# A quarter of each diagonal score block mirrored, mirrored tiles stored in twos, the stacked operand copied by GpSimd, and one router product two steps later

## Chip, cores and metric

The kernel runs on one core of a Trainium2 chip. The metric is the device time of one execution in microseconds (us), as the median of several runs.

## What is computed

The input is 8 batches of 1856 rows. An attention without softmax comes first, a mixture of 16 experts after it:

```python
scores = scale * np.matmul(z, z.transpose(0, 2, 1))     # z: 8 x 1856 x 64, scale = 1/1856
attn = np.maximum(scores, 0.0) ** 2
x = (u * np.matmul(attn, v)).reshape(14848, 256)
# router: best of 4 groups, then best of 4 experts in it, weight = both softmax values
# every row goes to its one expert e:
out[row] = weight * (np.maximum(x[row] @ w1[e], 0.0) @ w2[e])    # w1: 256 x 1024, w2: 1024 x 256
```

The matrix of scores is symmetric in each batch.

## The kernel before

**Tiles.** In each batch the 1856 queries are cut into four chunks, c = 0 to 3 (in batches 1 to 7: 512, 512, 512 and 320 wide), and the keys into 15 blocks of 128, k = 0 to 14 (the last has 64 new ones). One *step* is one key block of one chunk, so a batch has 60 steps. All fp32 values are split into a high and a low fp32r part, and each product is made of these parts.

**One step.** `scores(s)` makes the scores of a block: two matmuls (L365, L366) into one of three PSUM banks; ScalarE applies Relu (L369, tile `r`) and Square (L376); VectorE makes the high part `ah` (L377) and the low part `al` (L380). In steps that `ACT_TWICE` names, ScalarE squares twice and so makes `ah` as well (L373, L374), and VectorE's L377 falls away. `attn_v(s)` then has six matmuls (L402, L403, L405, two halves of the output's columns) that add `ah` and `al` times v to the output banks. `scores` runs six steps ahead of `attn_v` (`LEAD`). `zm` is the chunk's query operand: the high part of z in partitions 0 to 63, the low part in 64 to 127. It is put together in step 5 of the chunk before (L257) by two DMAs of the Sync queue, and has two buffers.

**Mirrored blocks.** In batches 1 to 7 a block below the diagonal is not computed. When a block above the diagonal is done, `put_mirror` (L302) transposes it in 32x32 tiles on VectorE (L305, tile `mt`) and the Sync queue stores it in DRAM (`sym`, L313). Seven steps before the mirrored block's turn, `load_mirror` (L315) loads four key blocks with four DMAs into an `at` tile (L321); ScalarE makes `ah` from it (L354) and VectorE `al` (L355). The order of the key blocks in a chunk stands in the table `KORD`. The diagonal blocks, key blocks 4c to 4c+3 of chunks 0 to 2, are computed whole.

**Buffers.** `r`, `ah`, `al`, `mt` and the parts of z share one ring `q` of 31 tiles of 2 KB per partition.

**Router.** At a chunk's end the product with u gives `xT`; `logits` (L472) makes the router's product on TensorE in PSUM tag `m`, which has one bank, `logits_out` (L480) empties it one step later, and `LG` (L492) says how many steps after the chunk's end this happens: 9 for the third chunk, which is step 8 of the fourth. The routing itself (`route`) is many small VectorE operations, a small product in the same bank `m` (L600), and scatters of rows into `bucket` by GpSimd's indirect DMAs (L637).

**Order.** From step 15 to step 464 TensorE, VectorE and ScalarE run their instructions in the order in which the program records them. The order of the Sync and GpSimd queues is set by a scheduler. Each engine works its queue in order. After step 479 come the 16 experts (`phase1`, `phase2_t`, L860), which the change doesn't touch.

Of the kernel before, what the change touches and what calls it, by code (L numbers as in the profile page):

```python
# [29 lines left out]
def tile_glu_attn_moe(  # L30
# [311 lines left out]
    def scores(s):  # L342
# [3 lines left out]
        for far in (ATL, 12):  # L346
            lb, lc, li = steps[min(s + far, NS - 1)]
            lk = key(lb, lc, li)
            if lk % KT == 0 and mirrored(lb, lc, lk) and ((lc, lk) == (3, 8) and lb < B - 1) == (far != ATL):
                load_mirror(lb, lk // KT, KB[lc])  # L350
        if mirrored(b, c, k):
            at = ats[(b, k // KT, KB[c])][:, k % KT]
            ah, al = new_z(f"ah_{s}")[:, 0:w], new_z(f"al_{s}")[:, 0:w]
            nc.scalar.copy(out=ah.rearrange("p (g x) -> p g x", x=32), in_=at)  # L354
            nc.vector.tensor_sub(  # L355
                out=al.rearrange("p (g x) -> p g x", x=32), in0=at, in1=f32(ah).rearrange("p (g x) -> p g x", x=32)
            )
# [891 lines left out]
```

## Time and profile before

| | |
|---|---|
| median of 3 runs | 1449.96 us (1449.88 to 1450.25) |
| the profiled execution's own time | 1449.4 us |
| its span, first to last instruction | 1447.6 us |
| mean granted TensorE clock | 0.998 of full speed |
| TensorE (PE) busy | 1436.9 us, 99% |
| VectorE (DVE) busy | 1137.4 us, 79% |
| ScalarE (ACT) busy | 926.1 us, 64% |
| GpSimd (POOL) busy | 284.3 us, 20% |
| DMA queue of Sync: share of the 16 DMA engines | 62.1% |

Busy time of TensorE counts pipelined matmuls, which overlap: one matmul's listed duration is longer than the distance from its start to the next one's. The attention takes the first 765 us or so, the experts the rest; shares over the whole span mix the two.

### The profile page before, as it was taken

To read this page: it belongs to the slowest core of one execution; us is meant where nothing else is said; L and a number is where in the kernel's file an instruction comes from. 1 tells how busy PE (TensorE), PEld (TensorE's weight loads), DVE (VectorE), ACT (ScalarE), POOL (GpSimd) and SP (SyncE) were. 2 spreads that over 40 slices of the span, in tenths; PEclk is the share of its full clock that TensorE was granted. 3 is DMA by queue.
4 is the path that set the end of the run, shared out by engine and by line. 5 is a ranking of instruction groups with operands and counts; after the bars stand their busy time and mean duration, and the time that the engine had idled before them with its cause. 6 is when DMAs were issued, how large, how long until landed. Compare 5 with 4: busy or idle time off the path is not lost.

```text
span 1447.6 us, 22265 instructions
## 1 busy us (share of the span) xinstructions
PE 1436.9 (99%) x7113; PEld 1240.4 (86%) x7113; DVE 1137.4 (79%) x2339; ACT 926.1 (64%) x1613; POOL 284.3 (20%) x351
## 2 busy tenths in 40 slices
PE   9999999999999999999999999999999999999997
PEld 7898888888888888888788999888888888999986
DVE  7889999999998998989988576776566666666663
ACT  8887887787878878778675354444445444444442
POOL 0002112220222203221114222111211221122122
PEclk9999999999999999999999999999999999999999
DMA  9997969979799797996975473554533545555421
GB/s 320 328 242 214 239 184 256 233 211 233 174 263 222 210 235 174 264 230 165 236 181 148 94 193 74 126 139 123 144 96 90 142 126 132 134 129 134 132 60 44
DMA packets 397656, 255.98 MB, mean 177 GB/s; under 512 B 241775, under 2 KB 352883, under 8 KB 397536
## 3 DMA queue, kind: packets, MB, share of 16 engines
q1 hardware_dynamic: 385712, 223.50, 62.1%
q0 software_dynamic: 11744, 30.90, 7.2%
q8 instruction: 56, 0.92, 0.3%
q14 instruction: 64, 0.52, 0.1%
q10 hardware_dynamic: 80, 0.13, 0.0%
HBM read 108.29 MB, written 89.21 MB: 136 GB/s over the span
## 4 chain that ended last, share of the span: by engine, by line
PE 99%; DVE 0%; ACT 0%; issue 0%; POOL 0%; POOLq 0%
PE yT L860 23%; PE o L402 14%; PE o L403 14%; PE o L405 13%; PE ph L787 8%; PE ph L786 8%; PE ph L788 8%; PE sc L365 5%; PE sc L366 5%; PE pl L478 1%; PE pl L477 1%; PE py L817 0%; PE warm_ps L913 0%; PE py L820 0%; PE pk L600 0%
## 5 line engine op out<-in xcount | busy, mean ns | idle before, releaser
L402 PE MATMUL o<-ah,vl 128*128 128x512 f32 (+2 forms) x960 | 354.4, 370 | 0.6 <-DVE ah L377 0.4
L403 PE MATMUL o<-ah,vh 128*128 128x512 f32 (+2 forms) x960 | 354.2, 369 | 0.0
L405 PE MATMUL o<-al,vh 128*128 128x512 f32 (+2 forms) x896 | 329.0, 369 | 0.0
L797 DVE SCALAR_TENSOR_TENSOR hl<-ph,hh 128x512 fp32r<-128x512 f32 (+12 forms) x288 | 173.8, 609 | 145.4 <-ACT hh L791 144.4
L860 PE MATMUL yT<-hh,w_e 128*128 128x512 f32 (+12 forms) x1120 | 269.3, 360 | 0.0
L791 ACT ACTIVATE hh<-ph 128x512 fp32r<-128x512 f32 (+12 forms) x288 | 153.5, 536 | 147.8 <-PE ph L788 144.9
L369 ACT ACTIVATE r<-sc 128x512 f32<-128x512 f32 (+2 forms) x312 | 178.6, 572 | 83.4 <-PE sc L366 80.4
L885 POOL DMA_INDIRECT out_dram<-y,meta x126 | 125.4, 995 | 496.4 <-DVE y L883 468.8
L860 PEld LDWEIGHTS yT<-hh,w_e 128*128 128x128 f32 x1120 | 200.1, 188 | 25.1
L637 POOL DMA_INDIRECT bucket<-rows,di x121 | 135.9, 1123 | 375.4 <-issue 217.3
L787 PE MATMUL ph<-xh_m,w1h_e 128*128 128x512 f32 (+12 forms) x576 | 207.3, 360 | 0.0
L402 PEld LDWEIGHTS o<-ah,vl 128*128 128x128 f32 x960 | 180.2, 188 | 30.6 <-DVE ah L377 0.8
L786 PE MATMUL ph<-xh_m,w1l_e 128*128 128x512 f32 (+12 forms) x576 | 206.4, 360 | 0.0
L403 PEld LDWEIGHTS o<-ah,vh 128*128 128x128 f32 x960 | 180.2, 188 | 29.0
L788 PE MATMUL ph<-xl_m,w1h_e 128*128 128x512 f32 (+12 forms) x576 | 202.8, 360 | 0.0
L380 DVE TENSOR_TENSOR al<-r,ah 128x512 fp32r<-128x512 f32 (+2 forms) x280 | 187.9, 671 | 17.3 <-PE sc L366 0.5
L405 PEld LDWEIGHTS o<-al,vh 128*128 128x128 f32 x896 | 167.9, 188 | 26.6 <-DVE al L380 0.7
L376 ACT ACTIVATE r<-r 128x512 f32<-128x512 f32 (+2 forms) x284 | 173.9, 612 | 9.0
L860 PE MATMUL yT<-hl,w_e 128*128 128x512 f32 (+12 forms) x560 | 159.1, 359 | 0.0
L863 ACT COPY yp<-yT 128x1024 uint16<-128x1024 uint16 (+2 forms) x70 | 59.3, 847 | 143.6 <-PE yT L860 104.9
L377 DVE CAST ah<-r 128x512 fp32r<-128x512 f32 (+2 forms) x284 | 117.8, 415 | 20.4 <-ACT r L376 14.6
L365 PE MATMUL sc<-zm,z2h 128*128 128x512 f32 (+2 forms) x312 | 120.1, 385 | 0.0
(164 smaller groups left out, 1964.3 us busy)
## 6 DMA issues: line engine op xcount, KB each, us to landing
raw_e<-in_w_dram SPq DMA_DIRECT2D x64, 512.0 KB, 6.4
sym<-mt SPq DMA_DIRECT2D x126, 256.0 KB, 4.2
at<-sym SPq DMA_DIRECT2D x84, 256.0 KB, 5.2
bucket<-padrow SPq DMA_DIRECT2D x32, 660.0 KB, 10.0
at<-sym SPq DMA_DIRECT2D x84, 160.0 KB, 5.9
vr<-in_v_dram SPq DMA_DIRECT2D x23, 512.0 KB, 5.3
ut<-in_uT_dram SPq DMA_DIRECT2D x23, 512.0 KB, 5.1
zr<-in_zT_dram SPq DMA_DIRECT2D x23, 256.0 KB, 8.6
```

What stands on the lines that cost most here:

```text
L365: held(nc.tensor.matmul(ps[:, 0:w], z2h[:, ks], zm, start=True, stop=False))
L369: held(nc.scalar.activation(out=a, in_=ps[:, 0:w], func=AF.Relu, scale=1.0 / S))
L376: held(nc.scalar.activation(out=a, in_=a, func=AF.Square))
L380: held(nc.vector.tensor_sub(out=al, in0=a, in1=f32(ah)))
L402: held(nc.tensor.matmul(o, vl[:, dsl], ah, start=(i == 0), stop=False))
L403: held(nc.tensor.matmul(o, vh[:, dsl], ah, start=False, stop=end and al is None))
L405: held(nc.tensor.matmul(o, vh[:, dsl], al, start=False, stop=end))
L786: nc.tensor.matmul(o, wt["l"][d][:, fs], xh[:, d, 0:W], start=(d == 0), stop=False)
L787: nc.tensor.matmul(o, wt["h"][d][:, fs], xh[:, d, 0:W], start=False, stop=False)
L788: nc.tensor.matmul(o, wt["h"][d][:, fs], xl[:, d, 0:W], start=False, stop=(d == ND - 1))
L797: nc.vector.scalar_tensor_tensor(out=dst, in0=o[:, c0:c1], scalar=0.0, in1=f32(hh[:, c0:c1]), op0=ALU.max, op1=ALU.subtract)
L860: nc.tensor.matmul(o, wt["2"][f // 2][:, w0:w0 + P], hs[f][q // 2][:, 0:n], start=((f, q) == (0, 0)), stop=((f, q) == (NF - 1, 2)))
```

## The change

Five things change together. The tables `KORD` and `ACT_TWICE` are new too; `ACT_TWICE` is now looked up by key block k, not by place in the chunk.

1. **Diagonal blocks.** In chunks 0 to 2 of batches 1 to 7, the third and fourth diagonal key blocks (k mod 4 = 2, 3) are computed for queries 256 to 511 of the chunk alone (`cut`, `w0`). Their first 256 columns are the mirror of what the first two diagonal blocks hold in columns 256 to 511. `put_diag` transposes that part (128x256) into a half of a `q` tile `dt`, and one DMA stores two of them (`dg`); `load_diag` loads them back, three steps ahead (`DGL`), with four DMAs into a tile `dl`. ScalarE and VectorE make `ah` and `al` from it in two more operations of 256 columns.
2. **Stores in twos.** Mirrored blocks with k below 12 are transposed into `st` tiles of 4 KB per partition, two blocks to a tile, and two such tiles exist (`NST`). One DMA of 512 KB stores both. Loads come in runs of 1 KB, not 512 bytes. Blocks 12 to 14 stay as they were.
3. **Ring.** The ring `q` has 27 tiles in place of 31.
4. **zm.** From chunk (1, 1) on, two GpSimd copies of 64 partitions put `zm` together, in place of two DMAs.
5. **Router.** `LG` of the third chunk is 11, not 9.

```diff
-    ACT_TWICE = ((4, 8, 12), (6, 10), (), ())
+    NST = 2
+    NQT = 27
+    ACT_TWICE = ((1, 6, 8, 9, 11), (5, 9, 12), (), ())
+    HALF = 256
+    DGL = 3
...
-                nc.sync.dma_start(f32(zm[0:DQ, dst]), f32(z2h[0:DQ, src]))
-                nc.sync.dma_start(f32(zm[DQ:P, dst]), f32(z2l[DQ:P, src]))
+                nc.gpsimd.tensor_copy(out=zm[0:DQ, dst], in_=f32(z2h[0:DQ, src]))
+                nc.gpsimd.tensor_copy(out=zm[DQ:P, dst], in_=f32(z2l[DQ:P, src]))
...
+    def put_duo(b, c, k, a):
+        cc, kk = k // KT, k % KT
+        pair = (b, KB[c], cc)
+        if (pair, kk % 2) not in duos:
+            duos[pair, kk % 2] = sb("st", [P, 1024], F32, NST, f"st_{b}_{c}_{k}").rearrange(
+                "p (j h t x) -> p h t j x", h=2, t=KT, x=32)
...
+        nc.vector.transpose(out=st[:, kk // 2], in_=a.rearrange("p (t j x) -> p t j x", t=KT, x=32))
+        if half:
...
+            nc.sync.dma_start(sym[pair][r0:r0 + P, :].rearrange("p (j h t x) -> p j h t x", h=2, t=KT, x=32),
+                              st.rearrange("p h t j x -> p j h t x"))
...
+    def half_diag(b, c, k):
+        return MB[0] <= b < MB[1] and c < NQ - 1 and k // KT == c
+
+    def put_diag(b, c, k, a):
...
+        t2 = dgs[(b, c)][:, kk * HALF:(kk + 1) * HALF]
+        nc.vector.transpose(
+            out=t2.rearrange("p (j t x) -> p t j x", t=2, x=32),
+            in_=a[:, HALF:512].rearrange("p (t j x) -> p t j x", t=2, x=32),
+        )
+        if kk == 1:
...
+            nc.sync.dma_start(
+                dgd[(b, c)].rearrange("(k p) w -> p k w", p=P),
+                dgs.pop((b, c)).rearrange("p (k w) -> p k w", k=2),
+            )
+
+    def load_diag(b, c):
+        at = new_zraw(f"dl_{b}_{c}").rearrange("p (g x) -> p g x", x=64)
+        src = dgd.pop((b, c)).rearrange("(g r) (j x) -> j r g x", r=32, x=64)
+        for j in range(4):
+            nc.sync.dma_start(at[j * 32:(j + 1) * 32], src[j])
...
     KORD = (
-        (0, 4, 1, 5, 2, 6, 3, 7, 8, 12, 9, 13, 10, 11, 14),
-        (0, 8, 1, 9, 2, 10, 3, 11, 4, 12, 5, 13, 6, 14, 7),
-        (12, 0, 13, 1, 14, 2, 8, 3, 9, 4, 10, 5, 11, 6, 7),
+        (0, 4, 1, 6, 5, 7, 8, 12, 10, 13, 2, 9, 3, 11, 14),
+        (4, 0, 5, 8, 1, 10, 2, 9, 3, 11, 12, 6, 13, 7, 14),
+        (8, 0, 9, 12, 1, 13, 2, 14, 3, 4, 5, 10, 6, 11, 7),
...
+        cut = half_diag(b, c, k) and k % KT >= 2
+        w0 = HALF if cut else 0
...
+        held(nc.tensor.matmul(ps[:, w0:w], z2h[:, ks], zm[:, w0:w], start=True, stop=False))
+        held(nc.tensor.matmul(ps[:, w0:w], z2l[:, ks], zm[:, w0:w], start=False, stop=True))
...
+        if half_diag(b, c, k) and k % KT < 2:
+            put_diag(b, c, k, a)
+        if cut:
+            at = dgs[(b, c)][:, k % KT - 2]
+            ag, lg = (x[:, 0:HALF].rearrange("p (g x) -> p g x", x=32) for x in (ahw, alw))
+            nc.scalar.copy(out=ag, in_=at)
+            nc.vector.tensor_sub(out=lg, in0=at, in1=f32(ag))
...
-        LG = (7 if b == B - 1 and c < 2 else (9 if c == 2 else 8 if c == 0 else 7)) if s + 1 < NS - NK else 2
+        LG = (7 if b == B - 1 and c < 2 else (11 if c == 2 else 8 if c == 0 else 7)) if s + 1 < NS - NK else 2
```

**TensorE**, chunk 0 of batch 4, where key block 2 is scored; step 246 before, step 250 after (`sc_250` is the bank of step 250). Before:

```order
L365 MATMUL sc_246_5061<-zm_4_0_4881,z2h_4_0_4609 128x512
L366 MATMUL sc_246_5061<-zm_4_0_4881,z2l_4_0_4610 128x512
L402 MATMUL o_4_0_0_5071<-ah_240_4946,vl_4_0_4127 128x512
L403 MATMUL o_4_0_0_5071<-ah_240_4946,vh_4_0_4126 128x512
L405 MATMUL o_4_0_0_5071<-al_240_4949,vh_4_0_4126 128x512
```

After:

```order
L438 MATMUL sc_250_5265<-zm_4_0_4971,z2h_4_0_4691 128x256
L439 MATMUL sc_250_5265<-zm_4_0_4971,z2l_4_0_4692 128x256
L486 MATMUL o_4_0_0_5167<-ah_244_5110,vl_4_1_4781 128x512
L487 MATMUL o_4_0_0_5167<-ah_244_5110,vh_4_1_4780 128x512
L489 MATMUL o_4_0_0_5167<-al_244_5113,vh_4_1_4780 128x512
```

The two score matmuls have half the columns, and the block stands four steps later in its chunk. In the whole program 84 matmuls are halved so (7 batches, 3 chunks, 2 blocks, 2 matmuls).

**VectorE**, the first steps of the same chunk (`xT` belongs to the chunk before). Before:

```order
L377 CAST ah_245_5033<-r_245_5031 128x512 [waits PE_49,Activation_49]
L380 TENSOR_TENSOR al_245_5036<-r_245_5031,ah_245_5033 128x512 [waits DVE_49]
L305 STREAM_TRANSPOSE mt_4_0_6_5038<-r_245_5031 128x4x4x32 [waits PE_49]
L424 TENSOR_TENSOR xT_3_3_5047<-o_3_3_0_4789,ut_3_3_4569 128x320 [waits PE_49]
L424 TENSOR_TENSOR xT_3_3_5047<-o_3_3_1_4790,ut_3_3_4569 128x320 [waits PE_49]
L377 CAST ah_246_5066<-r_246_5064 128x512 [waits Activation_49]
L380 TENSOR_TENSOR al_246_5069<-r_246_5064,ah_246_5066 128x512 [waits DVE_49]
```

After, from the transpose that fills the first `st` tile:

```order
L319 STREAM_TRANSPOSE st_4_0_4_5054<-r_243_5089 128x4x4x32
L451 CAST ah_244_5110<-r_244_5108 128x512 [waits PE_49,Activation_49]
L455 TENSOR_TENSOR al_244_5113<-r_244_5108,ah_244_5110 128x512 [waits DVE_49]
L319 STREAM_TRANSPOSE st_4_0_5_5115<-r_244_5108 128x4x4x32
L451 CAST ah_245_5128<-r_245_5126 128x512 [waits PE_49,Activation_49]
L455 TENSOR_TENSOR al_245_5131<-r_245_5126,ah_245_5128 128x512 [waits DVE_49]
L319 STREAM_TRANSPOSE st_4_0_5_5115<-r_245_5126 128x4x4x32
L508 TENSOR_TENSOR xT_3_3_5141<-o_3_3_0_4879,ut_3_3_4655 128x320 [waits PE_49]
L508 TENSOR_TENSOR xT_3_3_5141<-o_3_3_1_4880,ut_3_3_4655 128x320 [waits PE_49]
L455 TENSOR_TENSOR al_246_5163<-r_246_5158,ah_246_5160 128x512 [waits Activation_49]
L319 STREAM_TRANSPOSE st_4_0_8_5165<-r_246_5158 128x4x4x32 [waits DMAHW0_49]
```

The transpose into the third tile of the chunk (`st_4_0_8`) now waits for a DMA: the store of the first tile (`st_4_0_4`), whose buffer it takes.

**GpSimd**, from the end of batch 5 into batch 6 (`pl` and `lgp` are cleared tails of router tiles, `rows` the row tiles that are scattered). Before:

```order
L438 IOTA rows_5_3_7436 128x3x7
L451 MEMSET pl_5_3_7438 128x4x64
L452 MEMSET lgp_5_3_7439 48x2x64
L637 DMA bucket_69<-rows_5_0_6575,di_5_0_0_7491 246016x264 x4
L637 DMA bucket_69<-rows_5_1_6881,di_5_0_0_7491 246016x264 x4
L438 IOTA rows_6_0_7768 128x4x7
```

After:

```order
L522 IOTA rows_5_3_7590 128x3x7
L273 CAST zm_6_1_7736<-z2h_6_1_7255 64x512
L274 CAST zm_6_1_7736<-z2l_6_1_7256 64x512
L535 MEMSET pl_5_3_7592 128x4x64
L536 MEMSET lgp_5_3_7593 48x2x64
L721 DMA bucket_69<-rows_5_0_6707,di_5_0_0_7653 246016x264 x4
L273 CAST zm_6_2_8055<-z2h_6_2_7370 64x512
L274 CAST zm_6_2_8055<-z2l_6_2_7371 64x512
L721 DMA bucket_69<-rows_5_1_7026,di_5_0_0_7653 246016x264 x4
L522 IOTA rows_6_0_7930 128x4x7
```

The copies for chunks 1 and 2 of batch 6 stand among the scatters of batch 5; those of chunk 2 between the scatters of two row tiles.

## Rows read from the trace of the kernel before

**Rows 1.** The chain that ended last, shares of the span by engine.

```profile
PE 99%; DVE 0%; ACT 0%; issue 0%; POOL 0%; POOLq 0%
```

**Rows 2.** Window of batch 3: us, engines' busy time (instructions), clock, DMA, GB/s.

```profile
295.97:388.63 92.66, 92.66 (x450) 77.81 (x448) 86.15 (x189) 75.44 (x134) 19.57 (x22) 1.00 0.90 221
```

**Rows 3.** Experts in the chain (start us, us), timeline, weight loads.

```profile
792.12 10.88 PE yT L860 x48
...
839.42 5.76 PE yT L860 x48
...
839.26 1.36 PE L860 MATMUL yT<-hh,w_e 128*128 128x256 f32 x10
...
L860 PEld LDWEIGHTS yT<-hh,w_e 128*128 128x128 f32 x1120 | 200.1, 188 | 25.1
```

**Rows 4.** VectorE's groups by shape: count, busy us, mean ns of one, idle before.

```profile
L380 DVE TENSOR_TENSOR al<-r,ah 128x512 fp32r<-128x512 f32 x238 | 164.4, 691 | 14.2 <-PE sc L366 0.5
...
L305 DVE STREAM_TRANSPOSE mt<-r 128x512 f32<-128x512 f32 x147 | 103.6, 705 | 0.6
...
L377 DVE CAST ah<-r 128x512 fp32r<-128x512 f32 x233 | 99.6, 427 | 12.8 <-ACT r L376 8.4 <-DMA sym<-mt 2.4 <-ACT ah L354 0.6
...
L355 DVE TENSOR_TENSOR al<-at,ah 128x512 fp32r<-128x512 f32 x84 | 55.9, 672 | 0.7 <-DMA sym<-mt 0.6
...
L377 DVE CAST ah<-r 128x320 fp32r<-128x320 f32 x21 | 6.9, 331 | 2.5 <-ACT r L376 2.3
L380 DVE TENSOR_TENSOR al<-r,ah 128x320 fp32r<-128x320 f32 x14 | 6.9, 491 | 1.0
```

**Rows 5.** ScalarE's groups by shape, the same columns.

```profile
L354 ACT CAST ah<-at 128x512 fp32r<-128x512 f32 x84 | 51.1, 609 | 7.4 <-DMA sym<-mt 4.4 <-DVE ah L383 2.9 <-DMA at<-sym 0.2
...
L373 ACT ACTIVATE ah<-r 128x512 fp32r<-128x512 f32 x28 | 17.8, 634 | 0.9
```

**Rows 6.** Timeline around a scatter: start us, us, engine, line, operation.

```profile
312.24 0.96 POOL L637 DMA_INDIRECT bucket<-rows,di  x1 [0.30 <-issue]
...
312.88 0.55 DVE L377 CAST ah<-r 128x512 fp32r<-128x512 f32 x1
...
317.48 0.43 DVE L377 CAST ah<-r 128x512 fp32r<-128x512 f32 x1 [0.21 <-ACT r L376]
```

**Rows 7.** A GpSimd group; VectorE's copies into zm (ns min/median/max).

```profile
L132 POOL TENSOR_SCALAR_AFFINE_SELECT tri<-tri 128x128 bf16<-128x128 bf16 x1 | 0.3, 282 | 0.0
...
L266 DVE CAST zm<-z2h x5: 194/361/411, 21.3 to 99.5; 64x512 fp32r<-64x512 f32 x2, 64x416 fp32r<-64x416 f32 x1, 64x96 fp32r<-64x96 f32 x1, 64x320 fp32r<-64x320 f32 x1
```

**Rows 8.** DMA issues: number, KB each, median us from issue to landing.

```profile
raw_e<-in_w_dram SPq DMA_DIRECT2D x64, 512.0 KB, 6.4
sym<-mt SPq DMA_DIRECT2D x126, 256.0 KB, 4.2
at<-sym SPq DMA_DIRECT2D x84, 256.0 KB, 5.2
```

**Rows 9.** Timeline of ScalarE and TensorE at the end of batch 3.

```profile
382.57 0.99 ACT L485 COPY lgp<-pl 48x1024 uint16<-48x1024 uint16 x1
...
388.49 0.23 PE L600 MATMUL pk<-oh,tri 128*128 128x128 bf16 x1
```

**Rows 10.** Timelines of VectorE and TensorE, fourth chunk, batches 1, 3, 7.

```profile
196.84 0.49 DVE L355 TENSOR_TENSOR al<-at,ah 128x320 fp32r<-128x320 f32 x1
198.25 0.31 PE L402 MATMUL o<-ah,vl 128*128 128x320 f32 x1
...
380.27 0.49 DVE L355 TENSOR_TENSOR al<-at,ah 128x320 fp32r<-128x320 f32 x1
383.59 0.31 PE L402 MATMUL o<-ah,vl 128*128 128x320 f32 x1
...
753.77 0.49 DVE L355 TENSOR_TENSOR al<-at,ah 128x320 fp32r<-128x320 f32 x1 [0.75 <-ACT ah L354]
753.93 0.31 PE L402 MATMUL o<-ah,vl 128*128 128x320 f32 x1
```

More of the change, by code (lines that the diff above doesn't have):

```diff
@@ L104, in new_zraw @@
     def new_zraw(name):
-        return sb("q", [P, 512], F32, 31, name)
+        return sb("q", [P, 512], F32, NQT, name)
     def new_z(name):
-        return sb("q", [P, 512], F32R, 31, name)
+        return sb("q", [P, 512], F32R, NQT, name)
     def new_rows(name):
@@ L300, in mirrored @@
         return MB[0] <= b < MB[1] and KB[c] < MC and k // KT < MC and POS[k // KT] < c
+    duos = {}
+    def put_duo(b, c, k, a):
[4 more added lines that the diff above has]
+                "p (j h t x) -> p h t j x", h=2, t=KT, x=32)
+            half = 0
+        else:
+            half = 1
+        st = duos[pair, kk % 2]
+        nc.vector.transpose(out=st[:, kk // 2], in_=a.rearrange("p (t j x) -> p t j x", t=KT, x=32))
+        if half:
+            duos.pop((pair, kk % 2))
+            if pair not in sym:
+                sym[pair] = tc.dram_tile([2 * P, 1024], F32, name=f"sym_{b}_{c}_{cc}")
+            r0 = kk % 2 * P
+            nc.sync.dma_start(sym[pair][r0:r0 + P, :].rearrange("p (j h t x) -> p j h t x", h=2, t=KT, x=32),
+                              st.rearrange("p h t j x -> p j h t x"))
     def put_mirror(b, c, k, a):
+        if k // KT < NQ - 1:
+            put_duo(b, c, k, a)
+            return
         t2 = new_zraw(f"mt_{b}_{c}_{k}")
@@ L350, in scores @@
                 load_mirror(lb, lk // KT, KB[lc])
+        lb, lc, li = steps[min(s + DGL, NS - 1)]
+        lk = key(lb, lc, li)
+        if half_diag(lb, lc, lk) and lk % KT == 2:
+            load_diag(lb, lc)
         if mirrored(b, c, k):
@@ L353, in scores @@
             ah, al = new_z(f"ah_{s}")[:, 0:w], new_z(f"al_{s}")[:, 0:w]
[L354 to L357, printed above, removed]
+            ag, lg = (x.rearrange("p (h g x) -> p h g x", h=2, x=32) if c < NQ - 1 else
+                      x.rearrange("p (g x) -> p g x", x=32) for x in (ah, al))
+            nc.scalar.copy(out=ag, in_=at)
+            nc.vector.tensor_sub(out=lg, in0=at, in1=f32(ag))
             hl[s] = (ah, al)
@@ L363, in scores @@
         ps = bank(ps_s, "s", f"sc_{s}")
+        cut = half_diag(b, c, k) and k % KT >= 2
+        w0 = HALF if cut else 0
         held = pin if s < LEAD + NK else same
-        held(nc.tensor.matmul(ps[:, 0:w], z2h[:, ks], zm, start=True, stop=False))
-        held(nc.tensor.matmul(ps[:, 0:w], z2l[:, ks], zm, start=False, stop=True))
-        a = new_zraw(f"r_{s}")[:, 0:w]
+        held(nc.tensor.matmul(ps[:, w0:w], z2h[:, ks], zm[:, w0:w], start=True, stop=False))
+        held(nc.tensor.matmul(ps[:, w0:w], z2l[:, ks], zm[:, w0:w], start=False, stop=True))
+        a = new_zraw(f"r_{s}")[:, w0:w]
         held = pin if s < NK else same
-        held(nc.scalar.activation(out=a, in_=ps[:, 0:w], func=AF.Relu, scale=1.0 / S))
-        ah = new_z(f"ah_{s}")[:, 0:w]
+        held(nc.scalar.activation(out=a, in_=ps[:, w0:w], func=AF.Relu, scale=1.0 / S))
+        ahw = new_z(f"ah_{s}")[:, 0:w]
+        ah = ahw[:, w0:w]
         mirror = MB[0] <= b < MB[1] and KB[c] < MC and k // KT < MC and c < POS[k // KT]
-        if i in (ACT_TWICE[c] if MB[0] <= b < MB[1] else ()) and s >= NK:
+        if k in (ACT_TWICE[c] if MB[0] <= b < MB[1] else ()) and s >= NK:
             held(nc.scalar.activation(out=ah, in_=a, func=AF.Square))
@@ L378, in scores @@
         if k < NKF:
-            al = new_z(f"al_{s}")[:, 0:w]
+            alw = new_z(f"al_{s}")[:, 0:w]
+            al = alw[:, w0:w]
             held(nc.vector.tensor_sub(out=al, in0=a, in1=f32(ah)))
         else:
-            al = None
+            alw = None
             nc.vector.tensor_sub(out=ah[TAIL:P, :], in0=a[TAIL:P, :], in1=f32(ah[TAIL:P, :]))
@@ L385, in scores @@
             put_mirror(b, c, k, a)
-        hl[s] = (ah, al)
+        if half_diag(b, c, k) and k % KT < 2:
[3 more added lines that the diff above has]
+            ag, lg = (x[:, 0:HALF].rearrange("p (g x) -> p g x", x=32) for x in (ahw, alw))
+            nc.scalar.copy(out=ag, in_=at)
+            nc.vector.tensor_sub(out=lg, in0=at, in1=f32(ag))
+            if k % KT == 3:
+                dgs.pop((b, c))
+        hl[s] = (ahw, alw)
     def attn_v(s):
```

14 lines of the change are left out of this document (added).

## The prediction

> **What bounds the kernel now.** I read the chain of waits first: 99% of it is TensorE [rows 1]. That is a share over two phases, so I then cut out one whole batch of the attention, batch 3. There TensorE is busy in all of its 92.66 us, at a granted clock of 1.00; VectorE is busy for 86.15 us, ScalarE for 75.44, GpSimd for 19.57, and the DMA engines are 90% busy [rows 2]. So TensorE is the bound, and the second engine, VectorE, has 92.66 − 86.15 = 6.5 us of idle time per batch. Every microsecond that the change takes from TensorE comes back only as long as VectorE can follow, and the change takes from one and gives to the other.
>
> What lies between the two is a queue six steps deep (`LEAD`): a step of TensorE is 92.66/60 = 1.54 us. How far VectorE is ahead in its worst place, the fourth chunk, is read from the end of an `al` and the start of the first matmul of its step. In batch 3 `al` ends at 380.76 and the step begins at 383.59: 2.8 us ahead. In batch 1 it is 197.33 against 198.25, 0.9 us ahead; in batch 7 it ends at 754.26, when the step has already begun at 753.93, after VectorE waited 0.75 us for ScalarE [rows 10]. The steady batches have a small reserve, the first and the last none.
>
> The profiled execution's own time, 1449.4 us, is 0.56 below the median of the runs, 1449.96; I count differences against the median.
>
> **Halved score matmuls: −9.0 us.** A matmul's listed duration overlaps with the next one's, so the price is the distance between starts. In the experts the chain has 48 matmuls of 512 columns in 10.88 us, 0.2267 us each, and 48 of 256 columns (the timeline shows the shape) in 5.76 us, 0.120 us each, with a weight load for each [rows 3]. Halving saves 0.107 us. There are 84 of them: 84 × 0.107 = 8.96 us, 12 or 1.28 us in each of batches 1 to 7, so that a batch goes to 91.38 us. Nothing else of TensorE's work changes.
>
> **VectorE's work: about +1 us per batch.** From 512 and 320 columns of `al`, 691 and 491 ns, the slope is 1.04 ns a column; from the casts, 427 and 331, it is 0.5. A transpose of 256 columns is then 705 − 266 = 439 ns, and each of the three chunks gets two, +0.88. A cut block has a cast of 299, an `al` of 425 and one from `dl` of 672 − 266 = 406, together 1130 against 427 + 691 = 1118: nothing [rows 4]. Three chunks give +2.7. `ACT_TWICE` goes against it: ScalarE squares twice in 8 blocks of a batch, not 4 (28 such operations in seven batches before), and VectorE loses 4 × 0.427 = 1.7 [rows 4, 5]. Sum +1.0, or 87.2 of 91.4 us; 4.2 us idle are left of 6.5.
>
> **ScalarE: hidden.** 4 × 0.634 = 2.5 for the squares and at most 6 × 0.61 = 3.7 for copies out of `dl` [rows 5]: 81.6 at most in 91.4.
>
> **GpSimd's copies: unknown price.** There are eight per batch (54 in all). VectorE's own copies of this size have a median of 0.36 us; a GpSimd operation on 128 elements takes 0.28, four times that is 1.13 [rows 7]. I take 0.7, in between, so 5.6 us per batch on an engine that is busy for 20 of 92 [rows 2]. That is hidden: a `zm` buffer is free when the last scores of the chunk before the previous one are done and is needed a chunk later, some 23 us, and a copy stands behind a few scatters of about 1 us [rows 6].
>
> The question is what the copies do to VectorE. A cast that ran beside a scatter's issue on GpSimd took 0.55 us, one without 0.43 [rows 6]: a disturbance of 0.12. A copy moves data all the time it runs, so per copy VectorE loses between 0 and the copy's whole 1.13. I take 0.3, nearer to the row than to the whole: 2.4 us per batch, which leaves 1.8 idle.
>
> The Trainium skill speaks against this edit: in "SBUF — State Buffer", section "Who interferes with whom", VectorE and GpSimd share a pair of ports under an exclusive lock, held for a whole instruction, and VectorE's operations with two inputs in SBUF, such as `al`, are kept out while GpSimd reads there. By that, VectorE would stand still for a copy's whole time. The row of the cast shows a much smaller effect, but of an operation that doesn't copy, so no run here decides it.
>
> **Stores in twos: a wait of 0 to 1.6 us per batch.** The transpose into the third `st` tile of chunk 0 waits for the first tile's store. Between the two VectorE has two steps of cast, `al` and transpose (2 × 1.82), an `al` (0.69) and two operations for `xT` (at most 0.49 each, as an `al` of that width): 5.3 us [rows 4]. A store of 256 KB lands 4.2 us after its issue, a transfer of 512 KB in 6.4 [rows 8]; with some 0.5 us to the issue, the wait is 0 to 1.6. I take 0.8. Behind it in VectorE's queue stand the next cast and `al`, which TensorE needs four or more steps later, so it takes from the idle time, 1.0 us of which is left. The loads in runs of 1 KB move the same bytes. The DMA engines, at 90% and 221 GB/s [rows 2], lose the `zm` transfers (256 KB a chunk) and gain a store and a load of 256 KB in three chunks: +0.5 MB per batch, 2.5% of 20.5 MB. It would be 92% of the time, so I count nothing, with the late transfers below as the other end.
>
> **`dl` and the ring: nothing.** In chunk 0, key blocks 1 and 2 stand 8 steps apart, 12 us: five steps, 7.7 us, from store to load, against a landing of 4.2. The load has three steps, 4.6 us, against 4.2 to 5.2 [rows 8]: ScalarE may wait 0.6, three times a batch, in 9.8 us of idle time. A ring of 27 brings buffers back up to four tiles earlier, about two steps, and TensorE's lead is six steps.
>
> **Router at step 11: nothing.** The last `lgp` copy ends at 383.56 and the product `pk` in the same bank came at 388.49 [rows 9], 4.9 us later; two steps are 3.1 us. 1.8 us are left.
>
> **Where no reserve is: +1.4 us.** In batches 1 and 7 the margins of 0.9 and 0 must pay for about 2 us more of VectorE's work and waits before the fourth chunk's trough. I count 0.5 and 0.9.
>
> **Sum.** 1449.96 − 8.96 + 1.4 = 1442.4 us.
>
> **Rivals.**
>
> *VectorE binds in part* (0.16). The reserve is 4.2 − 0.8 = 3.4 us per batch without the copies' disturbance, 0.42 per copy. From there on each batch grows by 8d − 3.4 us when a copy costs VectorE d. For d between 0.45 and 0.6 the seven batches lose 1.4 to 9.8 us and the time is 1444 to 1452. For it: margins of 0 to 2.8 us are thin. Against it: the cast's 0.12.
>
> *VectorE becomes the bound* (0.11), the case on the other side. The place is VectorE's queue beside the copies, and the point from which it decides is d = 0.6, where 7 × (8 × 0.6 − 3.4) = 9.8 us eat up the gain. At d = 0.7, the copy's whole assumed time, it is 7 × 2.2 = 15.4: 1442.4 + 15.4 = 1457.8; at 0.65 it is 1455. This is what a lock would do. For it: a copy never stops reading, unlike the scatter in the rows. Against it: the copy would have to stop VectorE completely, and VectorE's casts went on beside GpSimd's work.
>
> *Halving doesn't halve* (0.06). A weight load takes 188 ns [rows 3]; if it were the floor, a halved matmul saved only 227 − 188 = 39 ns, 3.3 us in all, and the time would be 1449.96 − 3.3 + 1.4 = 1448.1. Against it stands the row of 256 columns at 0.120 with a load each.
>
> *Late transfers* (0.06). The DMA engines have little left, and `dl` comes in close to its use. If `dl` were 2 us late in each of 21 chunks and half of that showed through a lead with a reserve of 1 us, it would cost some 5 to 9 us: 1447 to 1451. Against it: ScalarE's wait is six steps ahead of TensorE.
>
> *The main case* (0.61): 1440.0 to 1445. Its lower end is a gain without new stalls, 1441.0, with 1 us of the stalls in batch 7 gone as well; its upper end has 2.6 us more in batches 1 and 7.
>
> **The numbers.** About 0.2% is what a measurement of this kernel can tell from no change: below 1447.1 is faster, above 1452.9 slower. Faster: 0.61 of the main case, 0.12 of the first rival, 0.03 of the late transfers, 0.76. Same: 0.04, 0.06 and 0.03, 0.13. Slower: 0.11. The range of 1440.0 to 1449.0 holds the main case but for a little, most of the first rival, the third, and part of the fourth: about 0.8.
>
> **What would show it.** Right: a steady batch of about 91.4 us with TensorE busy throughout, matmuls of 256 columns whose starts are 0.12 us apart, VectorE at 87 to 90 us of a batch, and `al` beside a GpSimd copy no more than 0.3 us longer than without. Wrong by the lock: `al`, transposes or casts of over 1.2 us beside the copies, TensorE waiting for `al`, batches of 93 us or more. Wrong by the stores: the transpose of the third `st` tile behind a wait of several us for a DMA. Wrong by the router: `pk` waiting for `lgp`. A copy on GpSimd of over 1.13 us, or a share of the DMA engines well above 0.90, would make the sum wrong in terms that I took as hidden.

## The result and the profile after

The changed kernel took 1464.3 us (median of 4 runs, 1463.36 to 1466.55), the kernel before 1450.11 us on the same chip (1449.88 to 1450.33): a ratio of 1.010, interval 1.0083 to 1.0118. It is 14 us slower where 7.5 us less were forecast. The profiled run has a span of 1462.2 us against 1447.6.

Where the 14.7 us of span came from is read from the step at which each batch begins. The windows below are, in the changed kernel, batch 0, batch 1, batches 2 to 6 in one, and batch 7 up to its last step (columns as in [rows 2]):

```profile
8.88:114.05 105.17, 103.03 (x494) 90.78 (x494) 90.93 (x187) 92.70 (x166) 2.91 (x6) 1.00 0.97 287
114.05:208.45 94.40, 92.76 (x448) 76.72 (x447) 85.73 (x193) 75.31 (x142) 24.41 (x30) 1.00 0.87 222
208.45:673.51 465.06, 460.65 (x2231) 384.28 (x2230) 436.92 (x976) 379.86 (x716) 120.41 (x150) 1.00 0.92 226
673.51:777.64 104.13, 98.48 (x449) 81.57 (x448) 89.34 (x214) 71.56 (x134) 19.83 (x27) 0.95 0.81 207
```

The same four stretches of the kernel before:

```profile
8.21:111.03 102.82, 102.64 (x494) 90.79 (x494) 89.05 (x183) 91.56 (x165) 1.64 (x4) 1.00 1.01 297
111.03:203.85 92.82, 92.82 (x447) 77.86 (x446) 86.06 (x189) 73.50 (x131) 18.45 (x22) 1.00 0.86 220
203.85:667.18 463.33, 463.33 (x2231) 389.08 (x2230) 432.08 (x938) 377.80 (x668) 94.50 (x111) 1.00 0.90 221
667.18:762.11 94.93, 94.07 (x448) 78.71 (x447) 87.19 (x203) 69.71 (x124) 16.97 (x22) 1.00 0.86 205
```

Batch 0, in which no block is halved, lost 2.35 us; batch 1 lost 1.6; batches 2 to 6 lost 1.7 where 6.4 were to be gained; batch 7 lost 9.2. VectorE has 87.4 us of work per batch (436.92 / 5), as forecast (87.2). But TensorE, which missed nothing in batches 2 to 6 and 0.9 us in batch 7, now stands still for 4.4 us in batches 2 to 6 and 5.6 in batch 7, and in batch 7 its granted clock is 0.95. The waits in batches 2 to 6 stand nearly all in the fourth chunks, where VectorE's margin was least, and are for its `ah` and `al`. The time lost is more than the 4.4 us: the listed duration of a matmul of 512 columns, 0.39 us, covers the first 0.16 of a wait, and behind a wait some starts of 320 columns are 0.25 us apart, not 0.15.

What the engines wait for, in the whole run (us in total, times, longest): ScalarE stands before the copies out of `dl` in 20 places for 56.7 us, 2.8 us each.

```profile
ACT ah L466 <- DMA dl<-dg: 56.7, 20, 4.9
ACT ah L427 <- DMA sym<-mt: 14.7, 5, 3.7
```

```profile
PE pk L684 <- ACT lgp L569: 4.7, 2, 3.0
PE o L486 <- DVE ah L451: 3.8, 5, 1.2
PE pl L561 <- ACT xh L514: 1.4, 1, 1.4
```

Chunk 1 of batch 7 shows what one such wait can do. ScalarE waits 2.57 us for `dl`; six operations later it copies `lgp`, 715.40 to 716.40:

```profile
712.92 0.41 ACT L466 CAST ah<-dl 128x256 fp32r<-128x256 f32 x1 [2.57 <-DMA dl<-dg]
713.23 0.59 ACT L442 ACTIVATE r<-sc 128x512 f32<-128x512 f32 x1
...
715.11 0.39 ACT L466 CAST ah<-dl 128x256 fp32r<-128x256 f32 x1
715.40 1.00 ACT L569 COPY lgp<-pl 48x1024 uint16<-48x1024 uint16 x1
```

TensorE's next product, `pk`, needs the bank that this copy empties, and waits 3.0 us for it (0.9 in the kernel before). After that the starts of 512 columns are 0.43 us apart, not 0.227:

```profile
716.45 0.22 PE L684 MATMUL pk<-oh,tri 128*128 128x128 bf16 x1 [3.00 <-ACT lgp L569]
...
717.61 0.63 PE L486 MATMUL o<-ah,vl 128*128 128x512 f32 x1
718.04 0.63 PE L487 MATMUL o<-ah,vh 128*128 128x512 f32 x1
716.60:720.00 3.40, 3.40 (x11) 2.72 (x10) 1.79 (x6) 2.12 (x3) 0.90 (x2) 0.50 1.02 226
```

The granted clock is 0.50 in these 3.4 us, the lower of the two levels (1.2 GHz). At the end of the batch, behind a wait of 1.4 us for `xh`, it is low again: 0.60 of full speed on average from 763.0 to 769.5, with a wait of 0.8 for `al` in that stretch. So in chunk 1 a late load costs twice, by the wait and by the clock behind it; that the waits at the end of the batch come from late loads isn't shown.

### The profile page after: what moved, and what is told of

Read it like the earlier page. It is cut to its first block, busy times and chain, and to the rows that moved or that the text cites. A ratio compares the mean times of both kernels' runs of the same rounds, so it can differ in the third digit from the quotient of the medians.

```text
span 1462.2 us, 22493 instructions
## 1 busy us (share of the span) xinstructions
PE 1439.2 (98%) x7113; PEld 1238.1 (85%) x7113; DVE 1144.9 (78%) x2395; ACT 933.1 (64%) x1683; POOL 322.8 (22%) x405
## 5 line engine op out<-in xcount | busy, mean ns | idle before, releaser
L455 DVE TENSOR_TENSOR al<-r,ah 128x512 fp32r<-128x512 f32 (+3 forms) x280 | 179.0, 639 | 18.9 <-ACT r L448 1.6
L442 ACT ACTIVATE r<-sc 128x512 f32<-128x512 f32 (+3 forms) x312 | 168.9, 541 | 28.8 <-PE sc L439 28.2
L450 ACT ACTIVATE r<-r 128x512 f32<-128x512 f32 (+3 forms) x256 | 147.2, 575 | 8.1
L870 PEld LDWEIGHTS ph<-xh_m,w1l_e 128*128 128x128 f32 x576 | 108.5, 189 | 13.5
L871 PEld LDWEIGHTS ph<-xh_m,w1h_e 128*128 128x128 f32 x576 | 108.7, 189 | 13.1
```

What stands on the lines that cost most here:

```text
L442: held(nc.scalar.activation(out=a, in_=ps[:, w0:w], func=AF.Relu, scale=1.0 / S))
L450: held(nc.scalar.activation(out=a, in_=a, func=AF.Square))
L870: nc.tensor.matmul(o, wt["l"][d][:, fs], xh[:, d, 0:W], start=(d == 0), stop=False)
L871: nc.tensor.matmul(o, wt["h"][d][:, fs], xh[:, d, 0:W], start=False, stop=False)
```

## The experiments

The chips differ: the kernel before took 1449.5 to 1450.1 us on three of them and 1453.7 to 1456.8 on three others; what was measured on those is marked with a star. So ratios stand beside the kernel before on the same chip, and small differences between chips aren't weighed. Windows of the kernel before are from the first chip throughout. The theory at first was: late loads of `dl` hold ScalarE and, behind it, VectorE. Its rival: VectorE is full with its own work and GpSimd's copies.

**One part of the change alone.** `b_half` has 84 halved matmuls and nothing else (the second product leaves out 256 columns of the diagonal blocks):

```diff
-        nc.tensor.matmul(ps[:, 0:w], z2l[:, ks], zm, ...)
+        nc.tensor.matmul(ps[:, w0:w], z2l[:, ks], zm[:, w0:w], ...)   # w0 = 256 in diagonal blocks
```

> The kernel before, with 84 score matmuls halved and nothing else: the second of the pair (the low part of z) has columns 256 to 511 alone in all four diagonal blocks of the three chunks, so the low part's product is left out in the other columns. TensorE as the bound with VectorE's idle time as reserve: 84 x 0.107 = 9.0 us less, a ratio of 0.993 to 0.995. If a halved matmul is held at the 188 ns of its weight load: 0.998. If VectorE or the transfers already hold the steady batch: 0.998 or more.

Measured*: 0.9952 (0.9936 to 0.9968), 6.8 us less; the forecast step was 9.0. Batch 3 shows it in full, 91.44 us with TensorE busy throughout; batch 7 took 98.29, against 94.93 in the trace of the kernel before:

```profile
294.20:385.64 91.44, 91.44 (x448) 76.96 (x447) 86.85 (x189) 75.07 (x135) 18.30 (x22) 1.00 0.88 225
662.46:760.75 98.29, 95.01 (x450) 77.78 (x448) 89.83 (x208) 70.69 (x126) 17.61 (x22) 1.00 0.83 200
```

That the halving makes batch 7 longer isn't shown by this: `b_zmpool` and `b_ring27` below, which halve nothing, took 97.32 and 98.02 us there on chips with a star.

`b_dveplus` adds the six transposes of 128x256 in a batch to the kernel before:

```diff
+            nc.vector.transpose(out=xdt[0][:, ...], in_=a[:, 256:512]...)   # k // KT == c, k % KT < 2
```

> The kernel before, with the six transposes of 128x256 in a batch that the change adds, into a tile that nobody reads, and nothing else of the change: 2.6 us more for VectorE per batch, 18 in all. If the whole idle time of VectorE in the trace (6.5 us per batch) is a reserve, or the 3.5 us of it in waits over 0.2 us, the ratio is 1.000 to 1.002. If those waits are forced and VectorE has about 1 us of reserve, 1.004 to 1.010.

Measured: 1.0011 (1.0002 to 1.0021). In batches 2 to 6 (the second line) VectorE has 439 us of work, 2 more than in the changed kernel, and TensorE misses nothing. There VectorE's work is no limit at this speed. In the batches without reserve it seems to cost: in this trace batch 1 (the first line) took 94.01 us, not 92.82, which is three quarters of what it lost in the changed kernel, and batch 7 took 95.99, not 94.93.

```profile
111.88:205.89 94.01, 93.13 (x447) 77.69 (x446) 87.87 (x194) 74.19 (x133) 19.68 (x23) 1.00 0.85 218
205.89:669.22 463.33, 463.33 (x2231) 389.04 (x2230) 439.13 (x968) 373.52 (x667) 94.37 (x110) 1.00 0.91 221
```

`b_zmpool` puts `zm` together with GpSimd in the kernel before (the two lines of the change):

> The kernel before, with zm put together by GpSimd's copies and nothing else. If GpSimd keeps VectorE out for a copy's whole time (0.64 us, eight in a batch, 5 us against 3.5 us of waits): 1.002 to 1.008. If a copy costs VectorE about 0.1 us, as the durations beside the copies in the changed kernel say: within 0.1% of 1.000.

Measured*: 1.0008 (0.9992 to 1.0023): nothing. `b_ring27` has the shorter ring alone (31 to 27 in both lines):

> The kernel before, with 27 tiles in the ring q and not 31, and nothing else. Short ring (ScalarE waits to write into a tile until the store of the mirrored block that it held has landed, seen as waits for the store of mt): the ratio is 1.003 to 1.012. If buffers are not what holds it: within 0.2% of 1.000.

Measured*: 1.0013 (1.0003 to 1.0022), 1 to 2 us: within the 0.2%, so alone the ring isn't what holds it.

**One part undone.** `fulldiag` computes the diagonal blocks whole (`half_diag` returns False):

> The changed kernel with whole diagonal blocks (no dt, dg and dl), so without the 9.0 us that the halved matmuls save. Late loads: TensorE's extra waits of 23 us go but for some 5 us, 1464.3 + 9 - 18 = 1455 us, between 1451 and 1458. Full VectorE: it loses 2.7 us of work per batch of which only what exceeded the reserve comes back, 1461 us or more.

Measured*: 1.003 (1.0019 to 1.0041), 2.8 us above the kernel before, in time between the two expected values. Its batches 2 to 6 took 464.22 us, where the kernel before has 463.33, but batch 7 took 101.30, not 94.93:

```profile
671.11:772.41 101.30, 96.67 (x450) 79.75 (x448) 88.06 (x203) 71.80 (x128) 20.39 (x27) 0.98 0.77 192
```

So in the steady batches the rest of the change costs little and the loss comes with the halved diagonal; in batch 7 most of the loss stands without it. How much of that is the chip's isn't known: the kernel before itself took 1456.82 us on this one. `zmdma` goes back to the two DMAs for `zm`:

> The changed kernel with zm put together by two DMAs again, not by GpSimd. Full VectorE: its operations beside the copies are 0.65 us per batch longer in all, 4.5 us in seven batches, which come back: 1458 to 1461 us. Late loads: within 1.5 us of the changed kernel's 1464.3, or slower where the transfers of zm stand ahead of those of dl in Sync's queue.

Measured*: 1.0166 (1.0131 to 1.02). With 1478.01 us it was slower than `lg9` (1465.74), the other version with one edit on that chip: more DMAs in Sync's queue made it slower, and GpSimd's copies help here. `lg9` (11 to 9 in the table of steps):

> The changed kernel with LG 9 for the third chunk again. If the later router product costs time where batch 1 begins (pk 1.85 us late behind lgp), this wait goes and the time is 1461 to 1463 us; if the two steps are hidden, 1464.3 within 1 us.

Measured*: 1.0063 (1.0039 to 1.0087). Which ratio the changed kernel has on that chip isn't known, so the whole isn't weighed; the wait at the end of batch 0 is. Batch 0 takes 102.82 us again, as in the kernel before, and 105.17 in the changed one:

```profile
8.47:111.29 102.82, 102.66 (x494) 90.78 (x494) 89.09 (x182) 91.87 (x165) 2.80 (x6) 1.00 0.99 293
```

**The load earlier.** `dgl6` loads `dl` six steps ahead, not three:

```diff
-    DGL = 3
+    DGL = 6
```

> The changed kernel with DGL 6 in place of 3, so that the mirrored diagonal part is loaded three steps (4.6 us) earlier. Late loads (ScalarE stands 56.7 us before 20 of 21 copies out of dl, 2.8 us each, and VectorE behind it): these waits fall below 10 us, most of TensorE's waits in the fourth chunks of batches 1 to 6 (9.5 us) and part of those in batch 7 go, and the time is 1447 to 1454 us. Full VectorE (its own work and GpSimd's copies set the batch, whatever ScalarE does): 1461 us or more.

Measured*: 1.0202 (1.0177 to 1.0227): much slower, against the theory in this form. ScalarE's wait for `dl` did fall, to 17.8 us. What rose is Sync's queue: the load (line 372) stands at its head until the store of `dt` has landed (11.0 us in the changed kernel), and the loads of mirrored blocks (381) until theirs have (11.9):

```profile
SPq L372 <- DMA dg<-dt: 45.7, 20, 5.2
SPq L381 <- DMA sym<-st: 35.3, 15, 5.5
```

Everything behind it in the queue is late; batches 2 to 6 took 486.6 us. The theory that was left is that the round trip costs as a whole, by its queue places and transfers too. `dlpool6` does the same from GpSimd's queue (`nc.gpsimd.dma_start` in `load_diag`):

> The changed kernel with the loads of dl issued by GpSimd, six steps ahead (DGL 6). In the kernel dgl6 the loads of dl stood 45.7 us at the head of Sync's queue, waiting for the store of dg to land, and everything behind them was late. If that is why the earlier load lost, here ScalarE's wait for dl falls below 15 us without it, and the ratio is 1.000 to 1.005; if the early load loses for another reason (buffers, DMA load), 1.010 or more.

Measured*: 1.0231 (1.0213 to 1.0249). The load is no earlier there: ahead of it GpSimd stood 32.9 us in two places for an operation of the routing, and ScalarE waited 55.5 us for `dl` in ten places between 210 and 670 us, 7.7 at most. So it tells nothing of Sync's queue.

**The changed kernel again, and its limits taken away one by one**, on one chip:

> The changed kernel once more, as the measure for the others on this chip: 1.010 times the kernel before, as measured first. If the chip matters (the kernel before took 1456.8 us on the chip of the first four runs, 1450.1 on the first chip) by late transfers, the ratio differs from 1.010 by more than 0.3%.

Measured: 1.0088 (1.0071 to 1.0105). `twice` takes casts from VectorE:

```diff
-    ACT_TWICE = ((1, 6, 8, 9, 11), (5, 9, 12), (), ())
+    ACT_TWICE = ((1, 6, 8, 9, 11), (5, 9, 12), (9, 12, 13, 10), (12,))
```

> The changed kernel with five more blocks in ACT_TWICE (four in the third chunk, one in the fourth): VectorE loses 4 casts of 0.43 and one of 0.33, 2.0 us in a batch, ScalarE gains five squares of 0.4 to 0.63. Full VectorE: a batch is shorter by up to the 2.0 us, at most down to 91.4, so the ratio falls by 0.5 to 0.9%. Late transfers, by ScalarE or by others: within 0.3% of the changed kernel, or slower, since ScalarE is behind its own waits.

Measured: 1.0098 (1.0076 to 1.0119). No gain, as late loads would have it. `nolatedl` takes ScalarE's wait away:

```diff
-        dgs[(b, c)] = at.rearrange("p g (t x) -> p t g x", t=2)
+        dgs[(b, c)] = dgs[(b, c)].rearrange("p (g x) -> p g x", x=64)...   # dt itself
```

> The changed kernel in which ScalarE and VectorE read the cut blocks' first half from the tile dt on chip, not from dl (so that half isn't the mirror); store and load of dg go on as before, and nobody waits for the load. If ScalarE's wait for dl (56.7 us in 20 places) sets TensorE's waits, the ratio to the kernel before falls from 1.010 to 1.003 or less. If VectorE is full with its own work, it stays within 0.3% of the changed kernel.

Measured: 1.0085 (1.0068 to 1.0101). Alone the wait for `dl` isn't it either, though batches 2 to 6 of the profiled run, the fastest of four, fall from 465.06 to 462.08 us. By its expectation this spoke for full VectorE, as `twice` spoke for late transfers. `twice_nolatedl` has both:

> The edits of nolatedl and twice together: the cut blocks' first half is read from dt on chip (not the mirror), and VectorE loses 2.0 us of casts per batch. Two limits side by side (ScalarE's wait for dl, and VectorE with less than 1 us of reserve; each edit alone left the other): the ratio falls to 0.995 to 1.002. If what holds the kernel is something else (the order of the key blocks, the stores in twos, the other transfers): 1.005 to 1.010, as each edit alone.

Measured*: 1.0063 (1.0044 to 1.0081). Two limits side by side were not enough either.

**Stores one by one.** `single` has the `mt` tiles for all mirrored blocks and 31 tiles in the ring again; `single_lg9_twice` adds the edits of `lg9` and `twice`; `all_off` reads `dt` on chip as well.

```diff
-        if k // KT < NQ - 1:
-            put_duo(b, c, k, a)
-            return
...
-    NQT = 27
+    NQT = 31
```

> The changed kernel with mirrored blocks stored and loaded one by one in mt tiles again, and 31 tiles in the ring; half diagonals, order of the key blocks, zm by GpSimd and LG 11 stay. Short ring or stores in twos as a limit: the waits for the store of mt go, and the ratio falls from 1.010 or 1.0088 to 1.004 or less. If the wait for dl and VectorE's work are all of it: 1.007 to 1.011.

> The kernel single with LG 9 and with the five more blocks in ACT_TWICE: of the limits found (buffers, VectorE's work, router, dl) only the wait for dl stays. If these limits stand side by side, each of the removed ones is worth 0.1 to 0.3%: a ratio of 0.997 to 1.003. If one alone sets the time and it is dl: 1.005 or more.

> The kernel single_lg9_twice with the cut blocks' first half read from dt on chip, so that nobody waits for dl (that half isn't the mirror). All limits off: the steady batches take 91.45 us and the ratio is 0.993 to 0.998, the gain of the halved matmuls. If it stays above 1.002, there is a limit that none of the edits touches, such as the order of the key blocks.

Measured*: 1.0171 (1.0153 to 1.0189), 1.0168 (1.015 to 1.0186), 1.0147 (1.0128 to 1.0166): all worse than the changed kernel's 1.010 and 1.0088, so this way of taking limits off put a larger one in. In `single` the load of a mirrored block (line 385) waits at the head of Sync's queue for its stores:

```profile
SPq L385 <- DMA sym<-mt: 45.3, 13, 6.6
```

In the changed kernel the same wait is 7.3 us in five places. In the kernel before it is 19.4 us in eleven, and TensorE missed nothing:

```profile
SPq L321 <- DMA sym<-mt: 19.4, 11, 3.2
```

So with the new order of the key blocks the stores in twos seem to be needed, and no cost; that this wait is what made the three slower is argued, not shown.

**The round trip left out.** `nodg` is `nolatedl` without the store of `dt` and the loads of `dl`; VectorE's and ScalarE's work stays. It also takes no tile of the ring for `dl`.

```diff
-            nc.sync.dma_start(dgd[(b, c)]..., dgs[(b, c)]...)
...
-        for j in range(4):
-            nc.sync.dma_start(at[j * 32:(j + 1) * 32], src[j])
```

> The kernel nolatedl without the store of dg and the loads of dl: the cut blocks' first half is read from dt on chip (not the mirror), and the round trip through DRAM is left out whole, 21 stores and 84 loads; VectorE's transposes, the order of the key blocks, the stores in twos, the ring, zm and LG 11 stay. If the round trip costs by its place in Sync's queue and its share of the DMA engines, beyond ScalarE's wait for it: a ratio of 0.996 to 1.002. If VectorE's work, the other transfers, batch 1's and batch 7's router products hold the rest: 1.004 to 1.009, as nolatedl's 1.0085.

Measured: 1.0022 (1.0012 to 1.0033), on a chip on which the kernel before took 1449.47 us, against 1.0085 with the transfers. The windows are batch 1, batch 3, batches 2 to 6 in one, and batch 7:

```profile
114.37:208.31 93.94, 92.97 (x447) 76.65 (x446) 85.81 (x191) 74.99 (x141) 24.32 (x30) 1.00 0.79 209
299.76:391.22 91.46, 91.46 (x448) 77.00 (x446) 87.75 (x195) 75.95 (x144) 24.34 (x31) 1.00 0.84 213
208.31:666.40 458.09, 457.80 (x2232) 384.86 (x2231) 438.16 (x978) 381.07 (x716) 119.14 (x150) 1.00 0.83 213
666.40:769.06 102.66, 96.80 (x450) 79.52 (x449) 89.80 (x214) 71.49 (x134) 19.65 (x27) 0.97 0.78 193
```

The steady batch takes 91.45 us (91.46 in batch 3) with TensorE busy throughout, the forecast being 91.38, and VectorE does the same work, 438 us. DMA is at 0.83 against 0.92 in the changed kernel. The spared ring tile is hardly the gain: ScalarE's copies of mirrored blocks wait 14.9 us for the store of `mt`, 14.7 in the changed kernel. Batch 1 and batch 7 gain little: 93.94 and 102.66 us, not 94.40 and 104.13.

`direct16_lg9` computes everything, but carries `dt` to `dl` on chip by sixteen DMAs:

```diff
+            for j in range(4):
+                for q in range(4):
+                    nc.sync.dma_start(at[j * 32:(j + 1) * 32, q:8:4], src[q * 32:(q + 1) * 32, :, j])
```

> The changed kernel with LG 9 and without DRAM between dt and dl: sixteen DMAs of 16 KB (32 partitions) carry each half from dt to a tile dl of its own as soon as the second transpose is done, and the ring has 26 tiles. No load waits for a store. If the round trip is what costs: ScalarE's wait for dl falls below 20 us and the ratio is 0.997 to 1.003. If the number of issues in Sync's queue is what delays (36 more in a batch, at 0.45 us each 16 us of that queue): the transfers behind them are late and the ratio is 1.008 or more.

Measured: 1.1189 (1.117 to 1.1208), much worse than either case. ScalarE's waits for these DMAs are 103 us in two lines of the code, and in batches 2 to 6 the DMA engines move 172 GB/s at a share of 0.68 (226 and 0.92 in the changed kernel).

```profile
L423 ACT CAST ah<-at 128x512 fp32r<-128x512 f32 x84 | 50.7, 613 | 90.3 <-DMA dl<-dt 58.3 <-DMA sym<-mt 30.3 <-DMA at<-sym 1.8
L462 ACT CAST ah<-dl 128x256 fp32r<-128x256 f32 x42 | 16.6, 395 | 48.0 <-DMA dl<-dt 45.0 <-DMA sym<-mt 3.0
229.40:817.62 588.22, 507.52 (x2231) 401.10 (x2230) 442.42 (x976) 382.01 (x716) 117.04 (x150) 0.93 0.68 172
```

Only `b_half` was faster than the kernel before, and it leaves out a part of the product; no version that computes the whole was.

## Why the prediction was wrong, step by step

**Right.** TensorE is the bound of the kernel before, and 12 halved matmuls are worth 1.28 us per batch: 91.45 us in `nodg`, 91.44 in `b_half`. In the changed kernel batch 2 took 91.93 and batch 5 92.21 us. Halving halves, so the rival "halving doesn't halve" falls. VectorE's added work was (436.92 - 432.08)/5 = 1.0 us per batch, as forecast, with transposes of 436 ns (439 estimated) and `al` from `dl` of 437 (406).

**VectorE and GpSimd.** Both rivals built on them fall as causes in the steady batches, where `nodg` has the same work and copies in 91.45 us; the second had only the direction right, slower. Two signs that I had given for the lock, TensorE waiting for `al` and batches of over 93 us, came without it, so they didn't tell the causes apart. A copy takes 742 and 788 ns of GpSimd on average (0.7 taken); one took 1.57 us. Beside one, `al` becomes longer: 0.91 and 0.99 us where the group's mean without is 0.69.

```profile
L273 POOL CAST zm<-z2h 64x512 fp32r<-64x512 f32 x20 | 14.8, 742 | 134.6 <-PE sc L439 129.2 <-DVE al L455 4.5 <-ACT r L442 0.2
L274 POOL CAST zm<-z2l 64x512 fp32r<-64x512 f32 x20 | 15.8, 788 | 63.2 <-DMA bucket<-rows,di 53.7 <-DVE vl L293 5.6 <-DVE z2l L254 2.1
321.69 0.64 POOL L273 CAST zm<-z2h 64x512 fp32r<-64x512 f32 x1
325.93 0.76 POOL L274 CAST zm<-z2l 64x512 fp32r<-64x512 f32 x1 [3.60 <-DMA bucket<-rows,di]
321.98 0.91 DVE L455 TENSOR_TENSOR al<-r,ah 128x512 fp32r<-128x512 f32 x1
326.25 0.99 DVE L455 TENSOR_TENSOR al<-r,ah 128x512 fp32r<-128x512 f32 x1
```

So these two took 0.22 and 0.30 us more beside copies of 0.64 and 0.76, no more than the 0.3 that I took. By the rule of "SBUF — State Buffer", section "Who interferes with whom", in the Trainium skill, `al` would be kept out until the copy ends, here 0.35 and 0.44 us after its start; the trace agrees in kind and shows two thirds of that. In the whole run 39 of 490 `al` met a copy and were 4.5 us longer in all than the mean of the others of their shape, 0.08 us per copy (an estimate from the trace). One, of 320 columns, took 0.90 us where the group's mean is 0.49, so my sign "no more than 0.3" didn't hold everywhere. `b_zmpool` shows that it doesn't reach the time.

**The stores in twos.** No wait (0.8 taken): the transposes into `st` have none before them in the whole run.

```profile
L319 DVE STREAM_TRANSPOSE st<-r 128x512 f32<-128x512 f32 x84 | 59.1, 703 | 0.0
```

**The step that failed: "`dl` and the ring: nothing".** I worked out chunk 0, took a wait of 0.6 us in ScalarE's idle time, and counted it three times. In chunk 0 that was nearly right: the wait was 0.0 to 1.8 us in the seven batches. In chunks 1 and 2, where the key blocks stand nine steps apart and not eight, it was 2.1 to 4.9. Batch 4, chunks 0, 1 and 2 (`dt` is done, `dg` stores it, `dl` loads it, `ah<-dl` needs it):

```profile
393.49 0.43 DVE L356 STREAM_TRANSPOSE dt<-r 128x256 f32<-128x256 f32 x1
393.95 0.39 SPq L362 DMA_DIRECT2D dg<-dt  x1
398.90 2.27 SPq L372 DMA_DIRECT2D dl<-dg  x4
403.29 0.41 ACT L466 CAST ah<-dl 128x256 fp32r<-128x256 f32 x1 [0.56 <-DMA dl<-dg]
...
415.52 4.62 SPq L549 DMA_TRANSPOSE rows<-pl  x3
418.77 0.43 DVE L356 STREAM_TRANSPOSE dt<-r 128x256 f32<-128x256 f32 x1
421.79 0.45 SPq L362 DMA_DIRECT2D dg<-dt  x1
427.93 1.84 SPq L372 DMA_DIRECT2D dl<-dg  x4
428.98 0.42 ACT L450 ACTIVATE r<-r 128x256 f32<-128x256 f32 x1
433.95 0.41 ACT L466 CAST ah<-dl 128x256 fp32r<-128x256 f32 x1 [4.55 <-DMA dl<-dg]
...
459.59 0.41 ACT L466 CAST ah<-dl 128x256 fp32r<-128x256 f32 x1 [3.76 <-DMA dl<-dg]
SPq L372 <- DMA dg<-dt: 3.2, 1, 3.2
```

In chunk 0 the store is issued as soon as `dt` is done. In chunk 1 it is issued 2.6 us later, behind the router's transposes and three loads in Sync's queue, and the load stands at the head of the queue for 3.2 us until that store has landed (the last line, from 424 to 430 us). The four issues take 1.84 us, which I left out though the diff names four DMAs, and ScalarE, which wanted `dl` at 429.4, goes on at 433.95, 4.2 us after the last issue; the loads' landing, with a median of 4.2 us, was as taken. So what the sum lacked is the place of store and load in one queue with all the others; counting steps of TensorE doesn't show it. It fits `dgl6` too, where the earlier load waited 45.7 us for its stores.

That wait alone isn't the price: without it (`nolatedl`) batches 2 to 6 were 3.0 us shorter, without the transfers (`nodg`) another 4.0, in one profiled run of each. The term "I count nothing" for 0.5 MB more per batch failed too, though the share of the DMA engines came out as worked out, 0.92: 21 stores and 84 loads have places in a queue in which a load waits at the head for its store (10.9 us in batches 2 to 6), and take a share of DMA engines that are 90% busy. Which of the two weighs more isn't settled. My rival of late transfers had the mechanism, at 0.06 and a price of 5 to 9 us. The price in batches 2 to 6 is 465.06 - 458.09 = 7.0; in the whole kernel it is 10 to 11, by the medians (14.2 and 13.4 us above the kernel before, and 3.4 in `nodg`). Its time, 1447 to 1451, was missed because other terms failed as well: without the round trip the kernel is 3.4 us slower where 9.0 were to be gained, so 12.4 us come from elsewhere.

**"Router at step 11: nothing"** failed at one place. The 1.8 us were worked out in a steady batch. At the end of batch 0 `pk` waited 1.69 us behind `lgp`, and batch 0 took 105.17 us in place of 102.82; in all four versions of the changed kernel with LG 9 it took 102.8.

**"Where no reserve is: +1.4 us"** was the right place and mis-sized most. Batch 1 went from 92.82 to 94.40, +2.9 against its share of 91.5, and batch 7 from 94.93 to 104.13, 10.5 against 93.65, where 0.5 and 0.9 stood. In batch 1 VectorE's added work is a likely cause: with the transposes alone (`b_dveplus`) it took 1.2 us more, in one trace. In batch 7 the longer wait for `lgp` (2.1 us more) and 3.4 us at half the clock make 3.8 of the loss, by an estimate from the rows above; the rest lies in the waits and the low clock at the end of the batch. Most of this stands without the wait for `dl`: `fulldiag` and `nodg` had 101.30 and 102.66 us there. In `nodg` VectorE waits for a store of `mt`, has then 10.1 us of work in 10.5, the routing's operations among it, and makes `xT` late; ScalarE stands 5.9 us for it, and behind that are the copies for the next `al`, for which TensorE waits:

```profile
721.29 0.43 DVE L441 CAST ah<-r 128x512 fp32r<-128x512 f32 x1 [1.58 <-DMA sym<-mt]
730.04 1.22 ACT L504 CAST xh<-xT 128x512 fp32r<-128x512 f32 x2 [5.86 <-DVE xT L498]
732.48 0.50 PE L479 MATMUL o<-al,vh 128*128 128x512 f32 x1 [1.98 <-DVE al L418]
```

Why it comes to that is open. One rival is untested: the new order of the key blocks, with its own `ACT_TWICE`, is in all fifteen traces of the changed kernel and its versions, and no run undoes it. Batch 7 took 99.7 us or more in each of them, and 94.9 to 98.3 in the five with the old order.

So the sum is: +2.4 for LG in batch 0, +2.9 in batch 1 and +8.1 in batches 2 to 6 (465.06 against 463.33 - 6.4), 7.0 of these by the round trip of the diagonal, +10.5 in batch 7, less 9.0 for the halved matmuls and 0.9 that the experts took less: 14.0 of the 14.7, and 0.7 lies ahead of the first step.

## What to carry to other kernels

A transfer that is added to a nearly full DMA system is to be costed from the first issue to the last landing, all its issues and what stands ahead of it included, at every place where it occurs and not at one, and also by what it delays; loading it earlier only moves the wait into the queue if its own store hasn't landed. When the bound engine's time is cut, what was just in time can become late, so the part that gains must be tested alone and with the transfers it brings. Look at the batches without reserve first: there a wait of 3 us in TensorE's queue also took the clock.

## What was not expected of the hardware

After a wait of 3.0 us TensorE ran at a granted clock of 0.50 for 3.4 us. Sixteen DMAs of 16 KB between tiles on chip, in place of one store and four loads through DRAM, made the kernel 11.9% slower, and each issue took 0.63 us (4.43 us for seven). A DMA issue of Sync in a chain of four takes 0.46 us, so four in a row take longer than one step. The kernel before, which the first chip repeats within 0.03%, took 0.2 to 0.5% longer on three others, and spread from 1451 to 1461 us there; no run shows why.
